# A gated linear attention with two expert stages on one core: VectorE's attention work of the first group behind the range reduction, and four smaller edits

## The chip, the core and the metric

The kernel runs on one core of a Trainium2 chip. The metric is the device time of one execution in microseconds (us). Five engines work side by side, each through its own queue in order: TensorE (PE in the profile, its weight loads as PEld), VectorE (DVE), ScalarE (ACT), GpSimd (POOL) and SyncE (SP, which issues most transfers). They meet through semaphores only.

## What is computed

Three stages follow each other: a linear attention with a decay for every key channel, an MLP with the gate h·cos(h), and a mixture of eight experts of which each token takes one. Queries, keys, values and decays are (4, 8, 768, 48); the MLP takes 3072 tokens of 384 channels to 2048 and back, an expert to 1024 and back.

```python
def _attn_ref(q, k, v, alpha):
    state = np.zeros((B, H, D, D))
    for t in range(S):
        state = alpha[:, :, t, :, None] * state + np.einsum('bhd,bhe->bhde', k[:, :, t], v[:, :, t])
        y[:, :, t] = np.einsum('bhd,bhde->bhe', q[:, :, t], state)

def _moe_ref(x, w_in, w_out):
    h = x @ w_in
    g = h * np.cos(h)
    return g @ w_out

def _moe2_ref(x, w_gate, w_output_gate, w1, w2):
    logits = x @ w_gate
    e_idx = np.argmax(logits, axis=1)
...
    for e in range(E):
        mask = e_idx == e
        h = np.maximum(x[mask] @ w1[e], 0.0)
        out[mask] = gate_w[mask, None] * eom[mask, e, None] * (h @ w2[e])
```

## The kernel before

**Units, groups and slots.** The sequence is cut into 6 chunks of 128 steps; with 4 batches this makes 24 units, u = 0 to 23, and four units with the same chunk form a group of 512 tokens. The MLP takes a group g in 16 slots, one for each block of 128 hidden channels, so there are 96 slots; J counts them from 0, and slot J belongs to group J // 16. While the MLP works on group g, the attention units of group g + 1 are computed between its steps. Units 0 to 4 are prepared by hand ahead of slot 0 (the head); "the first group" below is slots 0 to 15, in which units 5, 6 and 7 are prepared and in which VectorE also unpacks the 64-bit MLP weights.

**One slot.** The order is written out by hand. Slot J emits, in this order: the nine matmuls of `stage1` (L366, into `hp`, one of two PSUM buffers); place A; `nearest` (ScalarE, L373) and for the slot before `gated_halves` (ScalarE L391, GpSimd L392: `gh` and `gl`); place T; `turn` (VectorE L379, the range reduction, then ScalarE L380 and L381); place B; `gated` (VectorE L384, which frees `hp`); place P; the nine matmuls of `stage2` for slot J - 2 (L405, into `acc`); places C and D. The attention steps are put into these places by `at_slot(J, place, step, u)`; steps of one place run in the order of their registration, and each engine keeps the order in which its instructions were emitted.

**VectorE's attention steps of a unit.** `decay` (L142, L143: a scan of 128x520 that gives `w`), `recip` (L151, L152: a second scan), `k_left` and `k_right` (L169, L173), and `carry` (L184, which multiplies the stored total `wtot` into `dc`, and on ScalarE L186, which copies the new total over `wtot`). Unit 5 has its decay in slot 1 and its k steps and carry in slot 3, unit 6 in slots 4 and 6, unit 7 in slots 7 and 9. GpSimd multiplies the other halves of q (L160, L165) and scales the state (L193).

**Weight words.** In slots 0 to 13 `narrow` (place B, VectorE L334, L339, L343, each twice) makes fp32 words of two 128x384 blocks; in place A of the slot after, `halves` rounds each on ScalarE (L354) and subtracts on GpSimd (L355: `wil`, `wol`).

**The state update.** For units 0 to 19 `update` (L272) multiplies the transposed keys `ks` (128x112 weights) with four 128-column blocks of values; a block holds two heads of 48 columns, at columns 0 to 47 and 80 to 127, and 32 columns of zeros between them. Each of these fp32 matmuls stands twice in the trace.

**The experts.** An expert has 448 rows (the first: 256 early and then 192). `load_rows` loads them as tiles of 128 rows and a last one of 64, `rows_trans` (L629) transposes each tile in three column blocks, the last as 64x128 into 64 columns, and the products follow (L644, L658, L666). The next expert's `rows_trans` stands between the second products of the current one.

**Warming.** `warm(22)` issues 22 matmuls on zeros at the start, before the first unit's scores; `warm(9)` nine more between that unit's scores and its values.

Of the kernel before, what the change touches and what calls it, by code (L numbers as in the profile page):

```python
# [8 lines left out]
F32 = mybir.dt.float32  # L9
# [30 lines left out]
QO, KO, AO, VO = 0, 4 * C, 8 * C, 8 * C + 4 * 130 + 8  # L40
UCOL = VO + 4 * C
EARLY = 256
MAGIC = 1.5 * 2.0 ** 23
# [11 lines left out]
def kernel(  # L55
# [60 lines left out]

    def load_unit(u, parts=((0, UCOL),)):
        if u not in un:
            if u == B - 1:

                un[u] = tuple(x_p.tile([128, n], F32, tag=t, name="un") for n, t in ((AO, "xh"), (UCOL - AO, "xl")))
            else:
                t = u_p.tile([128, UCOL], F32, tag="un", name="un")
                un[u] = (t[:, 0:AO], t[:, AO:UCOL], t)
        for c0, c1 in parts:
            t, o = (un[u][2], 0) if len(un[u]) > 2 else (un[u][c0 // AO], c0 // AO * AO)
            nc.sync.dma_start(out=t[:, c0 - o:c1 - o], in_=units[u][:, c0:c1])

    def views(u):
# [4 lines left out]
            wt[u],  # L134
            av[:, VO - AO:].rearrange("p (a c) -> p a c", a=4),
        )
# [40 lines left out]
    def carry(u):  # L177
# [4 lines left out]
        if i > 0:  # L182
            dc_t[u] = d_p.tile([128, 4, 1], F32, tag="dc", name="dc")
            nc.vector.tensor_tensor(out=dc_t[u], in0=wb, in1=w[:, :, 64:65], op=ALU.mult)  # L184
        if i < NCH - 1:
            nc.scalar.copy(wb, w[:, :, 129:130])  # L186

# [78 lines left out]
    def update(u):  # L266
        if u // B == NCH - 1:
            return
        ks = sc_t[u][1]
        pp = (ps_a if u < B else ps_m).tile([128, 4, C], F32, tag="acc1" if u < B else "m", name="pp")  # L270
        for p in range(4):
            nc.tensor.matmul(  # L272
                out=pp[0:64 + D, p, :], lhsT=ks[:, p, :], rhs=views(u)[3][:, p, :],
                start=True, stop=True,
            )
        pp_t[u] = pp

    def update_out(u):
# [3 lines left out]
        pp = pp_t.pop(u)  # L282
        for p0, c0, v0 in ((0, 0, 0), (64, D, C - D)):
            m = state[b][p0:p0 + D, :, c0:c0 + D]
            pv = pp[p0:p0 + D, :, v0:v0 + D]
            if i == 0:
# [319 lines left out]
    def load_rows(e, r0, n, pool, tag):  # L606
# [9 lines left out]
        if rest:  # L616
            nc.vector.memset(xe[rest:128, full, DM:ROW], 0.0)
            after_sends(nc.sync.dma_start(out=xe[0:rest, full, :], in_=xs[r0 + full * 128:r0 + n, :]))
        return dict(e=e, n=n, tiles=tiles, xe=xe)

    def rows_trans(r, pool, th, tl):
# [3 lines left out]
        for k in range(KD):  # L625
            tp = ps_m.tile([128, 512], F32, tag="m", name="tp")[:, :n]
            for j, m in enumerate(r["tiles"]):
                o = j * 128
                nc.tensor.transpose(tp[:, o:o + m], r["xe"][0:m, j, k * 128:(k + 1) * 128], ident[0:m, 0:m])  # L629
            nc.scalar.copy(xh[:, k, :], tp)  # L630
# [100 lines left out]
    for u in range(GU, NU):  # L731
        J = NF * (u // GU - 1) + ((-2, 1, 4, 7) if u // GU == 1 else (-1, 2, 5, 7))[u % GU]
        at_unit[u] = J
        if u > GU:

            at_slot(max(J - 6, at_unit[u - 3] + 7 if u - 3 >= GU else 0), "A", load_unit, u)
            at_slot(J, "A", decay, u)
            at_slot(J, "D", q_right, u)
            at_slot(J, "B", recip, u)
            at_slot(J + 1, "D", q_left, u)  # L740
            at_slot(J + 2, "A", k_left, u, nc.vector)
            at_slot(J + 2, "A", k_right, u, nc.vector)
            at_slot(J + 2, "A", carry, u)
            at_slot(J + 2, "D", carry_state, u)
# [45 lines left out]
    with tc.manual_schedule():  # L790
        nc.scalar.activation(out=busy[:, 0:1], in_=halfpi, func=ACTF.Sin)
        warm(22)
        load_words(0, 0)
# [5 lines left out]
        def prepare(u):  # L799
# [6 lines left out]
            q_left(u, nc.vector)  # L806
            carry(u)

        prepare(0)
# [48 lines left out]
        k_right(4, nc.vector)  # L858
        carry(4)
        carry_state(4, nc.vector)  # L860
        nc.vector.tensor_copy(base, c_sb[:, CEB:CEB + E])
# [296 lines left out]
```

## Time and profile before

| | |
|---|---|
| median of 3 runs | 834.96 us (834.9 to 835.65) |
| the profiled execution | 836.24 us, of which the span from first to last instruction is 834.5 us |
| mean granted TensorE clock | 0.987 |
| busy share of the span: PE, PEld, DVE, ACT, POOL | 96%, 80%, 60%, 51%, 37% |

The profile shows one execution. Its own time is 1.28 us above the median, and 1.74 us of it lie outside of the span. A timeline row gives the start and the duration in us, the engine, the line, the operation, out<-in, the shape and the count of merged instructions, and in brackets the idle time ahead of it with what ended it. Matmul ends are modelled and overlap, so starts are what is compared there. The rows themselves stand below.

### The profile page before, as it was taken

The numbers are of one execution on the slowest core, as the hardware profiler recorded it, in microseconds if no ns is written. First come the engines' busy times: TensorE is split into PE (matmuls) and PEld (weight loads), VectorE is DVE, ScalarE is ACT, GpSimd is POOL, SyncE is SP. The second block draws the span as 40 slices with busy tenths as digits, with TensorE's granted clock in tenths as the row PEclk, the third lists the DMA queues.
The fourth block names the chain that finished last, engine by engine and source line by source line (L and its number), as shares of the span: only waits on it lengthen the run. The fifth ranks groups of instructions, "written<-read, shape, count | busy, mean of one in ns | idle before, by whom it ended". The sixth has DMA issues, their size and how long they took to land.

```text
span 834.5 us, 13942 instructions
## 1 busy us (share of the span) xinstructions
PE 797.1 (96%) x5415; PEld 671.7 (80%) x5415; DVE 500.4 (60%) x968; ACT 427.3 (51%) x782; POOL 311.4 (37%) x284
## 2 busy tenths in 40 slices
PE   8679799999999999999999999999999999999994
PEld 4457577788888888888878878889999999999994
DVE  7989998675467546763766335653764464454530
ACT  2355455754575457644665476564554453453420
POOL 3456557544355336443555333742000100101101
PEclk9998999999999999999999999999999999999998
DMA  9424443723201130123010002304753543533201
GB/s 336 162 98 165 165 165 105 256 59 113 73 2 52 71 122 0 52 70 123 1 52 30 30 1 77 115 1 146 232 160 104 166 140 110 167 123 117 78 11 36
DMA packets 46731, 85.22 MB, mean 102 GB/s; under 512 B 4136, under 2 KB 38216, under 8 KB 44096
## 3 DMA queue, kind: packets, MB, share of 16 engines
q1 hardware_dynamic: 43200, 74.67, 27.5%
q0 software_dynamic: 3456, 9.57, 3.1%
q8 instruction: 45, 0.74, 0.4%
q14 instruction: 30, 0.25, 0.1%
HBM read 69.01 MB, written 15.99 MB: 102 GB/s over the span
## 4 chain that ended last, share of the span: by engine, by line
PE 53%; issue 27%; DVE 10%; POOL 4%; ACT 2%; DMA 1%; POOLq 0%; SPq 0%; ACTq 0%; DVEq 0%
PE acc L405 21%; PE hp L366 21%; POOL out_dram L678 4%; DVE cv L334 2%; PE sc L200 2%; DVE cv L339 2%; PE yp L258 2%; PE yp L250 2%; PE pp L272 1%; DVE cv L343 1%; PE tp L429 1%; DVE t L384 1%; DVE w L143 1%; DVE t L379 1%; PE lp L461 1%
## 5 line engine op out<-in xcount | busy, mean ns | idle before, releaser
L392 POOL TENSOR_TENSOR gl<-t,gh 128x512 fp32r<-128x512 f32 x95 | 126.8, 1335 | 182.3 <-ACT gh L391 140.2
L373 ACT ACTIVATE t<-hp 128x512 f32<-128x512 f32 x96 | 57.3, 597 | 121.5 <-PE hp L366 110.6
L384 DVE TENSOR_TENSOR t<-hp,t 128x512 f32<-128x512 f32 x96 | 65.7, 684 | 88.1 <-ACT t L381 88.1
L379 DVE SCALAR_TENSOR_TENSOR t<-t,hp 128x512 f32<-128x512 f32 x96 | 65.7, 685 | 86.9 <-ACT t L373 86.6
L678 POOL DMA_INDIRECT out_dram<-ot,tk x32 | 30.9, 967 | 220.8 <-ACT ot L677 220.5
L658 PE MATMUL op<-h,hb 128*128 128x384 f32 x384 | 102.8, 340 | 0.0
L648 DVE SCALAR_TENSOR_TENSOR hb<-hp,hb 128x64 fp32r<-128x64 f32 (+3 forms) x136 | 45.3, 372 | 75.4 <-ACT hb L646 75.3
L405 PE MATMUL acc<-gh,woh 128*128 128x512 f32 x288 | 89.1, 416 | 0.0
L366 PE MATMUL hp<-xh,wih 128*128 128x512 f32 x288 | 84.3, 401 | 4.7 <-DVE t L384 2.9
L405 PE MATMUL acc<-gl,woh 128*128 128x512 f32 x288 | 84.4, 400 | 0.0
L405 PE MATMUL acc<-gh,wol 128*128 128x512 f32 x288 | 83.8, 399 | 0.0
L366 PE MATMUL hp<-xh,wil 128*128 128x512 f32 x288 | 83.5, 398 | 0.0
L366 PE MATMUL hp<-xl,wih 128*128 128x512 f32 x288 | 83.4, 398 | 0.0
L380 ACT ACTIVATE t<-t 128x512 f32<-128x512 f32 x96 | 60.7, 632 | 34.8 <-DVE t L379 34.8
L586 DVE TENSOR_TENSOR l<-raw,h 128x768 fp32r<-128x768 f32 x60 | 57.3, 957 | 32.5 <-ACT h L582 31.1
L646 ACT ACTIVATE hb<-hp 128x448 fp32r<-128x448 f32 (+2 forms) x72 | 36.3, 504 | 71.6 <-PE hp L644 71.5
L381 ACT ACTIVATE t<-t,halfpi 128x512 f32<-128x512 f32 x96 | 69.6, 725 | 3.1
L658 PEld LDWEIGHTS op<-h,hb 128*128 128x128 f32 x384 | 69.9, 188 | 0.5
L366 PEld LDWEIGHTS hp<-xh,wih 128*128 128x128 f32 x288 | 54.1, 190 | 19.6 <-DVE t L384 2.0
L366 PEld LDWEIGHTS hp<-xl,wih 128*128 128x128 f32 x288 | 54.7, 190 | 13.4
L405 PEld LDWEIGHTS acc<-gl,woh 128*128 128x128 f32 x288 | 54.7, 190 | 13.2
L366 PEld LDWEIGHTS hp<-xh,wil 128*128 128x128 f32 x288 | 54.5, 189 | 13.2
(139 smaller groups left out, 1501.6 us busy)
## 6 DMA issues: line engine op xcount, KB each, us to landing
raw<-in_w_dram SPq DMA_DIRECT2D x64, 384.0 KB, 3.2
un<-in_units_dram SPq DMA_DIRECT2D x20, 1032.0 KB, 5.1
raw<-in_w_in_dram SPq DMA_DIRECT2D x16, 384.0 KB, 3.6
raw<-in_w_out_dram SPq DMA_DIRECT2D x16, 384.0 KB, 4.0
xs<-zrow SPq DMA_DIRECT2D x8, 591.0 KB, 5.9
xe<-xs SPq DMA_DIRECT2D x7, 591.0 KB, 5.6
un<-in_units_dram SPq DMA_DIRECT2D x4, 512.0 KB, 6.0
un<-in_units_dram SPq DMA_DIRECT2D x4, 264.0 KB, 5.1
```

The costliest lines, as they stand in the source:

```text
L366: nc.tensor.matmul(out=hp, lhsT=w[:, k, fs], rhs=x[:, k, :], start=(n == 0), stop=(n == 3 * KD - 1))
L373: nc.scalar.activation(out=t, in_=hps[g, j], func=ACTF.Copy, bias=MAGIC)
L379: nc.vector.scalar_tensor_tensor(out=t, in0=t, scalar=MAGIC, in1=hp, op0=ALU.subtract, op1=ALU.subtract)
L380: nc.scalar.activation(out=t, in_=t, func=ACTF.Abs)
L381: nc.scalar.activation(out=t, in_=t, func=ACTF.Sin, scale=-TWO_PI, bias=halfpi)
L384: nc.vector.tensor_tensor(out=t, in0=hps.pop((g, j)), in1=t, op=ALU.mult)
L392: eng.tensor_tensor(out=gl, in0=gf, in1=gh.bitcast(F32), op=ALU.subtract)
L405: nc.tensor.matmul(out=acc[g][k], lhsT=w[:, j, ks], rhs=a, start=(j == 0 and n == 0), stop=(j == NF - 1 and n == 2),)
L586: (nc.vector.tensor_tensor if i < 4 else sub)(out=lo, in0=raws[i], in1=h.bitcast(F32), op=ALU.subtract)
L648: nc.vector.scalar_tensor_tensor(out=out_, in0=hp[:, c], scalar=0.0, in1=hh[:, c].bitcast(F32), op0=ALU.max, op1=ALU.subtract)
L658: nc.tensor.matmul(out=op, lhsT=a[:, sl], rhs=w[:, j, :], start=(j == 0 and i == 0), stop=(j == NEF - 1 and i == 2))
L678: sent = nc.gpsimd.indirect_dma_start(out=out, out_offset=bass.IndirectOffsetOnAxis(ap=tk[0:n, t, :], axis=0), in_=ot[0:n], in_offset=None ...
```

## The change

Five edits. **Place:** for units 5, 6 and 7 `decay`, `k_left`, `k_right` and `carry` move from place A to place B, that is from ahead of `turn` to right behind it; later groups keep place A. **Decay copy:** ScalarE's copy into `wtot` leaves `carry` and becomes `carry_keep`, for the planned units in place C of the same slot. **Warming:** `warm(22)` becomes `warm(17)`. **Update:** the value blocks are read as two pieces of 48 columns (a view of 160 columns in two strides of 80), so the matmul streams 96 columns for 128, and `pp` is 96 wide; the unit's tile grows by 32 unused columns, so that the last view fits. **Transposes:** the last tile of an expert is transposed as full 128x128 too; its rows 64 to 127 are set to zero over the full width of 394 columns, where before only 10 columns of them were.

```diff
--- before.py
+++ after.py
@@ -39,6 +39,8 @@
 
 QO, KO, AO, VO = 0, 4 * C, 8 * C, 8 * C + 4 * 130 + 8
 UCOL = VO + 4 * C
+
+UPAD = UCOL + C - 2 * D
 EARLY = 256
 MAGIC = 1.5 * 2.0 ** 23
 TWO_PI = 2.0 * math.pi
@@ -118,10 +120,10 @@
         if u not in un:
             if u == B - 1:
 
-                un[u] = tuple(x_p.tile([128, n], F32, tag=t, name="un") for n, t in ((AO, "xh"), (UCOL - AO, "xl")))
+                un[u] = tuple(x_p.tile([128, n], F32, tag=t, name="un") for n, t in ((AO, "xh"), (UPAD - AO, "xl")))
             else:
-                t = u_p.tile([128, UCOL], F32, tag="un", name="un")
-                un[u] = (t[:, 0:AO], t[:, AO:UCOL], t)
+                t = u_p.tile([128, UPAD], F32, tag="un", name="un")
+                un[u] = (t[:, 0:AO], t[:, AO:UPAD], t)
         for c0, c1 in parts:
             t, o = (un[u][2], 0) if len(un[u]) > 2 else (un[u][c0 // AO], c0 // AO * AO)
             nc.sync.dma_start(out=t[:, c0 - o:c1 - o], in_=units[u][:, c0:c1])
@@ -132,7 +134,7 @@
             qk[:, QO:QO + 4 * C].rearrange("p (a c) -> p a c", a=4),
             qk[:, KO:KO + 4 * C].rearrange("p (a c) -> p a c", a=4),
             wt[u],
-            av[:, VO - AO:].rearrange("p (a c) -> p a c", a=4),
+            av[:, VO - AO:UCOL - AO].rearrange("p (a c) -> p a c", a=4),
         )
 
     def decay(u):
@@ -182,8 +184,11 @@
         if i > 0:
             dc_t[u] = d_p.tile([128, 4, 1], F32, tag="dc", name="dc")
             nc.vector.tensor_tensor(out=dc_t[u], in0=wb, in1=w[:, :, 64:65], op=ALU.mult)
+
+    def carry_keep(u):
+        b, i = u % B, u // B
         if i < NCH - 1:
-            nc.scalar.copy(wb, w[:, :, 129:130])
+            nc.scalar.copy(wtot[b].rearrange("p (a c) -> p a c", c=1), views(u)[2][:, :, 129:130])
 
     def carry_state(u, eng=nc.gpsimd):
         b, i = u % B, u // B
@@ -267,10 +272,12 @@
         if u // B == NCH - 1:
             return
         ks = sc_t[u][1]
-        pp = (ps_a if u < B else ps_m).tile([128, 4, C], F32, tag="acc1" if u < B else "m", name="pp")
+        pp = (ps_a if u < B else ps_m).tile([128, 4, 2 * D], F32, tag="acc1" if u < B else "m", name="pp")
         for p in range(4):
+            o = VO - AO + p * C
+            v = un[u][1][:, o:o + 2 * (C - D)].rearrange("p (n c) -> p n c", n=2)[:, :, 0:D]
             nc.tensor.matmul(
-                out=pp[0:64 + D, p, :], lhsT=ks[:, p, :], rhs=views(u)[3][:, p, :],
+                out=pp[0:64 + D, p, :], lhsT=ks[:, p, :], rhs=v,
                 start=True, stop=True,
             )
         pp_t[u] = pp
@@ -280,9 +287,9 @@
         if i == NCH - 1:
             return
         pp = pp_t.pop(u)
-        for p0, c0, v0 in ((0, 0, 0), (64, D, C - D)):
+        for p0, c0 in ((0, 0), (64, D)):
             m = state[b][p0:p0 + D, :, c0:c0 + D]
-            pv = pp[p0:p0 + D, :, v0:v0 + D]
+            pv = pp[p0:p0 + D, :, c0:c0 + D]
             if i == 0:
                 nc.scalar.copy(m, pv)
             else:
@@ -614,7 +621,7 @@
             out=xe[:, 0:full, :], in_=xs[r0:r0 + full * 128, :].rearrange("(j p) c -> p j c", p=128)
         ))
         if rest:
-            nc.vector.memset(xe[rest:128, full, DM:ROW], 0.0)
+            nc.vector.memset(xe[rest:128, full, :], 0.0)
             after_sends(nc.sync.dma_start(out=xe[0:rest, full, :], in_=xs[r0 + full * 128:r0 + n, :]))
         return dict(e=e, n=n, tiles=tiles, xe=xe)
 
@@ -623,10 +630,11 @@
         xh = pool.tile([128, KD, n], F32R, tag=th, name="exh")
         xl = pool.tile([128, KD, n], F32R, tag=tl, name="exl")
         for k in range(KD):
-            tp = ps_m.tile([128, 512], F32, tag="m", name="tp")[:, :n]
-            for j, m in enumerate(r["tiles"]):
-                o = j * 128
-                nc.tensor.transpose(tp[:, o:o + m], r["xe"][0:m, j, k * 128:(k + 1) * 128], ident[0:m, 0:m])
+
+            tp = ps_m.tile([128, 512], F32, tag="m", name="tp")
+            for j in range(len(r["tiles"])):
+                nc.tensor.transpose(tp[:, j * 128:(j + 1) * 128], r["xe"][:, j, k * 128:(k + 1) * 128], ident)
+            tp = tp[:, :n]
             nc.scalar.copy(xh[:, k, :], tp)
             nc.vector.tensor_tensor(out=xl[:, k, :], in0=tp, in1=xh[:, k, :].bitcast(F32), op=ALU.subtract)
         r["x"] = (xh, xl)
@@ -734,13 +742,17 @@
         if u > GU:
 
             at_slot(max(J - 6, at_unit[u - 3] + 7 if u - 3 >= GU else 0), "A", load_unit, u)
-            at_slot(J, "A", decay, u)
+
+
+            pl = "B" if u // GU == 1 else "A"
+            at_slot(J, pl, decay, u)
             at_slot(J, "D", q_right, u)
             at_slot(J, "B", recip, u)
             at_slot(J + 1, "D", q_left, u)
-            at_slot(J + 2, "A", k_left, u, nc.vector)
-            at_slot(J + 2, "A", k_right, u, nc.vector)
-            at_slot(J + 2, "A", carry, u)
+            at_slot(J + 2, pl, k_left, u, nc.vector)
+            at_slot(J + 2, pl, k_right, u, nc.vector)
+            at_slot(J + 2, pl, carry, u)
+            at_slot(J + 2, "C", carry_keep, u)
             at_slot(J + 2, "D", carry_state, u)
         at_slot(J + 3, "P", scores, u)
         at_slot(J + 3, "C", masked, u, 0)
@@ -789,7 +801,7 @@
 
     with tc.manual_schedule():
         nc.scalar.activation(out=busy[:, 0:1], in_=halfpi, func=ACTF.Sin)
-        warm(22)
+        warm(17)
         load_words(0, 0)
         load_words(0, 1)
         load_words(0, 2)
@@ -805,6 +817,7 @@
             k_right(u, nc.vector)
             q_left(u, nc.vector)
             carry(u)
+            carry_keep(u)
 
         prepare(0)
         scores(0)
@@ -857,6 +870,7 @@
         k_left(4, nc.vector)
         k_right(4, nc.vector)
         carry(4)
+        carry_keep(4)
         carry_state(4, nc.vector)
         nc.vector.tensor_copy(base, c_sb[:, CEB:CEB + E])
         nc.vector.tensor_copy(tri16, c_sb[:, CT:CT + 128])
```

**VectorE, slots 3 and 4** (`t<-t,hp` is `turn`, `t<-hp,t` is `gated`, `cv` are the words of `narrow`). Before, from behind slot 2's `gated` on:

```order
L169 TENSOR_TENSOR un<-un,w 128x4x64
L173 TENSOR_TENSOR un<-un 128x4x64
L184 TENSOR_TENSOR dc<-wtot_126,w 128x4
L379 SCALAR_TENSOR_TENSOR t<-t,hp 128x512
L334 TENSOR_SCALAR cv<-raw 128x384 x2
L339 SCALAR_TENSOR_TENSOR cv<-raw,cv 128x384 x2
L343 SCALAR_TENSOR_TENSOR cv<-raw,cv 128x384 x2
L384 TENSOR_TENSOR t<-hp,t 128x512
L304 SCALAR_TENSOR_TENSOR xl<-yp,xh 128x3x128
L142 MEMSET scan_120 128x8
L143 SCALAR_TENSOR_TENSOR w<-un,scan_120 128x520
```

Of the changed kernel, from the same place:

```order
L386 SCALAR_TENSOR_TENSOR t<-t,hp 128x512
L171 TENSOR_TENSOR un<-un,w 128x4x64
L175 TENSOR_TENSOR un<-un 128x4x64
L186 TENSOR_TENSOR dc<-wtot_126,w 128x4
L341 TENSOR_SCALAR cv<-raw 128x384 x2
L346 SCALAR_TENSOR_TENSOR cv<-raw,cv 128x384 x2
L350 SCALAR_TENSOR_TENSOR cv<-raw,cv 128x384 x2
L391 TENSOR_TENSOR t<-hp,t 128x512
L311 SCALAR_TENSOR_TENSOR xl<-yp,xh 128x3x128
L386 SCALAR_TENSOR_TENSOR t<-t,hp 128x512
L144 MEMSET scan_120 128x8
L145 SCALAR_TENSOR_TENSOR w<-un,scan_120 128x520
```

The k steps and `dc` of unit 5 now stand behind `turn` of slot 3, and the memset and scan of unit 6 behind `turn` of slot 4.

**ScalarE, from slot 3 to the start of slot 4** (`wih`, `woh` are the rounded weights, `t<-hp` is `nearest`). Before:

```order
L186 COPY wtot_126<-w 128x4
L354 CAST wih<-cv 128x3x128
L354 CAST woh<-cv 128x384
L373 ACTIVATE t<-hp 128x512
L391 CAST gh<-t 128x512
L380 ACTIVATE t<-t 128x512
L381 ACTIVATE t<-t,halfpi 128x512
L303 ACTIVATE xh<-yp 128x3x128
L354 CAST wih<-cv 128x3x128
L354 CAST woh<-cv 128x384
```

Of the changed kernel:

```order
L361 CAST wih<-cv 128x3x128
L361 CAST woh<-cv 128x384
L380 ACTIVATE t<-hp 128x512
L398 CAST gh<-t 128x512
L387 ACTIVATE t<-t 128x512
L388 ACTIVATE t<-t,halfpi 128x512
L310 ACTIVATE xh<-yp 128x3x128
L191 COPY wtot_126<-w 128x4
L361 CAST wih<-cv 128x3x128
L361 CAST woh<-cv 128x384
```

The copy into `wtot` went from ahead of slot 3's weight casts and `nearest` to the slot's end.

**TensorE, an expert's transposes** between its second products. Before:

```order
L629 MATMUL tp<-c_sb,xe 128x128 x3
L629 MATMUL tp<-c_sb,xe 128x64
L629 MATMUL tp<-c_sb,xe 128x128 x3
L629 MATMUL tp<-c_sb,xe 128x64
L629 MATMUL tp<-c_sb,xe 128x128 x3
L629 MATMUL tp<-c_sb,xe 128x64
L658 MATMUL op<-h_5169,hb 128x384
```

Of the changed kernel:

```order
L674 MATMUL op<-l_5165,hb 128x384
L636 MATMUL tp<-c_sb,xe 128x128 x12
L666 MATMUL op<-h_5164,hb 128x384
L666 MATMUL op<-l_5165,hb 128x384
L666 MATMUL op<-h_5164,hb 128x384 x2
```

Twelve transposes of one shape stand where three runs of three were each followed by a smaller one.

## Rows read from the trace of the kernel before

**Rows 1.** The page: the span.

```profile
span 834.5 us, 13942 instructions
```

**Rows 2.** Stretches: busy of PE, PEld, DVE, ACT, POOL (instructions); granted clock, DMA share, GB/s.

```profile
54.30:108.30 54.00, 43.65 (x299) 34.33 (x297) 49.01 (x86) 26.56 (x53) 32.59 (x29) 0.91 0.41 142
...
108.30:135.00 26.70, 26.03 (x176) 20.79 (x176) 25.84 (x45) 16.75 (x31) 16.31 (x15) 1.00 0.57 199
...
152.00:480.00 328.00, 328.00 (x2595) 265.82 (x2595) 194.51 (x365) 184.84 (x331) 153.57 (x134) 1.00 0.19 65
585.00:815.00 230.00, 229.45 (x1236) 215.06 (x1236) 116.09 (x255) 104.27 (x189) 26.00 (x27) 1.00 0.41 126
```

**Rows 3.** The same view: two stretches with a lower granted clock.

```profile
38.13:41.54 3.41, 3.41 (x9) 2.22 (x7) 3.37 (x7) 1.95 (x5) 1.80 (x2) 0.50 0.31 83
...
96.16:99.57 3.41, 3.41 (x10) 2.67 (x9) 3.41 (x8) 1.77 (x3) 1.37 (x2) 0.50 0.91 372
```

**Rows 4.** Timeline of the head.

```profile
7.08 0.89 DVE L165 TENSOR_TENSOR un<-un 128x252 f32<-128x252 f32 x1
...
7.40 1.84 PEld L717 LDWEIGHTS <-busy 128*128 128x128 bf16 x9 [0.27 <-issue]
...
10.86 1.29 DVE L219 TENSOR_TENSOR at<-sc,mask 128x512 f32<-128x512 f32 x2 [1.58 <-PE sc L200]
```

**Rows 5.** Timeline from the end of slot 5 into slot 6.

```profile
76.93 0.68 DVE L384 TENSOR_TENSOR t<-hp,t 128x512 f32<-128x512 f32 x1
...
78.38 0.20 ACT L186 COPY wtot<-w 128x4 f32<-128x4 f32 x1 [2.67 <-DVE dc L184]
...
79.94 0.69 DVE L379 SCALAR_TENSOR_TENSOR t<-t,hp 128x512 f32<-128x512 f32 x1 [1.59 <-ACT t L373]
```

**Rows 6.** Timeline of slot 12, a slot with no step in place A.

```profile
120.52 0.69 DVE L379 SCALAR_TENSOR_TENSOR t<-t,hp 128x512 f32<-128x512 f32 x1 [0.47 <-ACT t L373]
```

**Rows 7.** Timeline of slot 4.

```profile
63.60 1.00 POOL L355 TENSOR_TENSOR wol<-cv,woh 128x384 fp32r<-128x384 f32 x1
...
63.61 2.08 DVE L143 TENSOR_TENSOR_SCAN w<-un,scan 128x520 f32<-128x520 f32 x1
64.56 2.21 POOL L392 TENSOR_TENSOR gl<-t,gh 128x512 fp32r<-128x512 f32 x1
...
66.43 1.44 DVE L152 TENSOR_TENSOR_SCAN un<-un,scan 128x520 f32<-128x520 f32 x1
```

**Rows 8.** Timeline of slot 1.

```profile
41.69 0.60 ACT L373 ACTIVATE t<-hp 128x512 f32<-128x512 f32 x1 [1.56 <-PE hp L366]
```

**Rows 9.** Timeline of slot 17.

```profile
150.69 0.14 PEld L429 LDWEIGHTS tp<-c_sb,xh 128*128 128x128 f32 x1 [0.32 <-ACT xh L418]
```

**Rows 10.** Timeline: an update and what follows; then weight loads by form: busy, mean ns, idle before.

```profile
215.05 1.04 PE L272 MATMUL pp<-un,ks 128*112 128x128 f32 x8
215.85 0.71 PE L405 MATMUL acc<-gh,woh 128*128 128x512 f32 x2
...
L366 PEld LDWEIGHTS hp<-xh,wil 128*128 128x128 f32 x288 | 54.5, 189 | 13.2
...
L258 PEld LDWEIGHTS yp<-at,un 128*32 128x32 f32 x768 | 21.5, 110 | 4.5 <-DVE at L219 4.1 <-issue 0.4
L272 PEld LDWEIGHTS pp<-un,ks 128*112 128x112 f32 x160 | 19.9, 176 | 6.5 <-ACT ks L224 4.2 <-issue 0.6
```

**Rows 11.** Timeline of an expert's transposes, and of twelve full-size ones.

```profile
620.83 2.05 PE L629 MATMUL tp<-c_sb,xe 128*128 128x128 f32 x12
622.81 0.45 PE L658 MATMUL op<-h,hb 128*128 128x384 f32 x1
...
565.02 1.61 PE L429 MATMUL tp<-c_sb,xh 128*128 128x128 f32 x12
566.47 0.18 PE L504 MATMUL rp<-oh,tri 128*128 128x32 bf16 x1
```

**Rows 12.** Timeline of the start: a memset of 128x520.

```profile
0.93 0.49 DVE L704 MEMSET scan<- 128x520 f32 x1 [0.93 <-PEq L1147]
```

## The prediction

> **What bounds the kernel now.** I read the span [rows 1] and then the table by stretches [rows 2]. From 152 us on TensorE never stands: 328.00 us busy of 328.00, and 229.45 of 230.00 in the experts. There every column or idle gap taken from TensorE shortens the span, and what VectorE does is covered (194.51 of 328.00, 116.09 of 230.00). From 54.3 to 108.3 us it is the other way round: VectorE is busy 49.01 of 54.00 us and TensorE 43.65, so a slot lasts as long as VectorE's row with its waits. From 108.3 to 135 us both are full (25.84 and 26.03 of 26.70). So there are three accounts: the head, the first group by VectorE, and the rest by TensorE.
>
> **Warming, five matmuls fewer.** The last nine warming loads start within 7.40 to 9.24 us, 0.20 us each [rows 4], and five of them are 1.0 us. The last operand of the first scores that VectorE makes is ready at 7.08 + 0.89 = 7.97 us, and VectorE then idles 1.58 us until those scores are there [rows 4]. The gap is longer than the piece cut out, so all of 1.0 us should move on through the head, in which VectorE goes from one unit to the next; **-1.0 us**, with 0 and -1.1 as ends. The five are those at the faster pace, behind the point at which the clock is up, so no slower matmul is added.
>
> **The decay copy and the k steps, slots 3, 6 and 9.** In slot 6 `gated` starts at 76.93 and `turn` at 79.94 us, 3.01 us later, and VectorE idles 1.59 us of that for ScalarE's `nearest` [rows 5]. ScalarE is late because its copy into `wtot` waits 2.67 us for `dc`, that is for VectorE's k steps, and the weight casts and `nearest` are queued behind the copy. In slot 12, with nothing in place A, the same wait is 0.47 us [rows 6]. With the copy at the slot's end and the k steps behind `turn`, slots 3, 6 and 9 should wait as slot 12 does: 1.59 - 0.47 = 1.1 us less each. The k steps themselves (some 0.8 us) are moved, not removed. They now stand where GpSimd runs `wil`, `wol` and `gl`, and rows of slot 4 show what that means [rows 7]: the scan that is issued at 63.61, just behind `wol` at 63.60, takes 2.08 us and ends 1.1 us behind `wol`, and `gl` then takes 2.21 us. One waits for the other, instruction by instruction. But the unpacking that followed `turn` before already waited for the same GpSimd work; the k steps take its place in that wait. I price the contention as unchanged; if it is all new, it eats the 1.1 us, which is the other end. In slot 9 TensorE may be late too: the clock was at 0.50 from 96.16 to 99.57 us [rows 3], which is where `hp` of slot 9 is made, so I take 0.7 there. Sum: **-2.9 us**, from 0 to -3.3.
>
> **The decays, slots 1, 4 and 7.** In slot 4 the scan stood ahead of `turn` and spent its first 0.9 us waiting for `wol` [rows 7]. Behind `turn` it is issued about 0.7 us later and still finds `wol` only just done, so it ends where it did; the second scan (66.43, 1.44 us) then waits for `gl`, which ends at 64.56 + 2.21 = 66.77 us, as before. Slots 4 and 7: 0. Slot 1 is different. There ScalarE's `nearest` waits 1.56 us for TensorE's `hp` [rows 8], because TensorE runs at half clock from 38.13 us [rows 3]; the scan fills that wait now, and behind `turn` it will not. That costs up to 1.4 us, and nothing if the clock comes back in time; **+0.7 us**.
>
> **Slot 17.** The same copy stands ahead of `nearest` there, and two transposes wait for ScalarE's copies out of `acc`, one of them 0.32 us in the weight load [rows 9], the other about as much. With `nearest` some 0.7 us earlier and the copy's own 0.2 us behind, about 0.5 us of both goes: **-0.5 us**. In the later groups the copy blocks ScalarE too, but TensorE does not stand, so it is worth 0.
>
> **The update.** Eight fp32 matmuls (four, each twice) take 215.85 - 215.05 = 0.80 us, 0.10 each [rows 10]. If the moving columns set this, 96 for 128 saves a quarter, 0.2 us. If the weight loads do, it saves less: a load lasts 110 ns for 32 columns, 176 for 112 and 189 for 128, so 0.8 ns per column, and the 112 columns are 0.09 us of streaming, nearly the whole 0.10. I lean to the loads, since their slope is the nearest row, and take 0.06 us. Units 8 to 19 do it in the TensorE-bound part, 12 times: **-0.7 us**, from 0 to -2.4; units 0 to 7 lie under VectorE. The Trainium skill, page "TensorE: Matmul & The Clock Gate", section "LDWEIGHTS (loading the stationary operand)", puts a load at its columns divided by 1.2 ns, whatever its rows; 112 columns are 93 ns by that, and it speaks against a full quarter here. The slope of the three rows agrees with it; taken as the floor of a matmul's spacing, it would leave an estimate of 12 x 8 x 7 ns = 0.7 us.
>
> **The transposes.** Twelve, of which three are 64-row tiles, take 622.81 - 620.83 = 1.98 us; twelve full ones elsewhere take 566.47 - 565.02 = 1.45 us [rows 11]. So the small tiles cost more than full ones, 0.53 us in an expert. Seven experts give 3.7 us, and the first one's later rows, with three small tiles among six, about the same 0.5: **-4.2 us**. The ends are -5.2 (the spacing within a run of full tiles is a little lower) and 0 (if the step to the next PSUM tile, not the tile's height, is what costs). They stand on TensorE between second products, with TensorE full [rows 2]. The wider memset replaces a small one; one of 128x520 took 0.49 us [rows 12], it is issued an expert ahead, and VectorE is half idle there: 0. Without that cover it would cost 8 x 0.4 us.
>
> **Sum.** -1.0 - 2.9 + 0.7 - 0.5 - 0.7 - 4.2 = -8.6 us, so the profiled span of 834.5 would be 825.9 and its 836.24 us would be 827.6. The median, 834.96, lies 1.28 us under the profiled execution; from it, **826.4 us**. Differences below 0.2% (1.7 us) can hardly be told from no change here.
>
> **The rivals.**
> (a) The first group gives nothing. For it: the k steps meet GpSimd's row, TensorE is full from 108 us on and may hold the slots where VectorE no longer does, and slot 1 loses its cover. Against it: the idle 1.59 us has one clear cause. Then -1.0 - 0.7 - 4.2 = -5.9: 829.1 us.
> (b) Everything at its good end: moving columns set the update (-2.4), the clock is back in slots 1 and 9 (-3.3, 0), transposes -5.2. With the head and slot 17, -12.4: 822.6 us. For it: the spacing within a run of transposes; against: the slope of the loads.
> (c) The transposes gain nothing. For it: the three groups of an expert also change PSUM tile. Against it: the twelve full ones change it too and are faster. Then -4.4: 830.6 us.
> (d) Slower: the clock. It fell to 0.50 in the first 100 us [rows 3], and these stretches lay in the part that VectorE paces. If the new order shifts TensorE's idle gaps so that the clock falls in the stretch where TensorE is full, each us at 0.50 there costs half a us. It decides from 2 x 8.6 = 17 us at the lower level; 21 us give 836.9. In the three stretches from 108 us on the clock is 1.00 [rows 2], so this is unlikely.
> (e) The change does not do what it says, because VectorE's waits for GpSimd and not ScalarE's copy set the slots: that is (a) in its price.
>
> **How the numbers follow.** Forecast (group gains between half and full) 0.55; (a) with (e) 0.20; (b) 0.12; (c) 0.08; (d) 0.03; no visible change from a mix of losses 0.02. The range takes in (a) and the near side of (b): 822.8 to 829.6 us. Faster by over 0.2% is the forecast, (a), (b) and (c), 0.95; I give 0.94 to that, 0.03 to within 0.2% and 0.03 to slower.
>
> **What would show it.** Per step: the first scores 1.0 us earlier; in slots 3, 6 and 9 about 1.9 us from `gated` to `turn` less, with VectorE's idle before `turn` near 0.5 us, and the copy into `wtot` without its wait; in slots 4 and 7 the same length as before; in slot 1 an idle VectorE ahead of `turn`; eight update matmuls in 0.6 to 0.75 us; twelve transposes in 1.3 to 1.5 us. Wrong would be slots 3, 6 and 9 as long as before, longer waits in the unpacking, or transposes of 1.9 us.

## The result, and the profile after

The changed kernel takes 824.31 us (median of 4 runs, 824.0 to 827.59) where the kernel before takes 835.26 us beside it; the ratio is 0.988, 95% interval 0.985 to 0.990. In a second set of runs the same kernel measured 827.14 us (5 runs, 823.52 to 827.71) against 835.5: 0.989, 0.987 to 0.991. The nine runs lie on two levels, four at 823.5 to 824.5 with a mean granted clock of 0.987 to 0.989, and five at 827.1 to 827.7 with 0.982 to 0.985; a section below shows, for one execution of each level, which slots make the 3 us. The forecast was 826.4 us, 822.8 to 829.6.

The profiled execution took 824.48 us; its page's span answers [rows 1]:

```profile
span 822.6 us, 13914 instructions
```

The stretches that answer [rows 2], moved to the same work (busy time of PE, PEld, DVE, ACT and POOL with their instructions, then granted clock, DMA share and GB/s):

```profile
54.00:104.00 50.00, 42.33 (x331) 33.48 (x324) 48.25 (x84) 25.98 (x50) 32.30 (x28) 0.96 0.44 154
104.00:131.00 27.00, 25.85 (x180) 20.73 (x179) 26.16 (x47) 17.40 (x32) 16.24 (x15) 1.00 0.56 196
148.00:476.00 328.00, 328.00 (x2601) 265.81 (x2601) 195.79 (x366) 184.81 (x332) 153.56 (x134) 1.00 0.19 66
580.00:803.00 223.00, 222.70 (x1233) 214.18 (x1234) 116.02 (x254) 102.44 (x188) 26.38 (x27) 1.00 0.43 131
```

The three accounts still hold: VectorE paces the first stretch (48.25 of 50.00 us), TensorE the last two. Set against each other work by work, the two traces give the ledger of the profiled pair:

| place | shift of the changed kernel, us | its own part |
|---|---|---|
| `gated` of slot 0 | -0.46 | head -0.5 |
| `gated` of slot 10 | -2.70 | first group -2.2 |
| `turn` of slot 19 | -3.44 | slot 17 -0.9, then +0.1 |
| `turn` of slot 95 | -4.61 | updates -1.2 |
| last matmul | -11.62 | experts -7.0 |
| last instruction | -11.85 | end -0.2 |

**Slot 6**, `gated` of slot 5 to the copy, answers [rows 5]:

```profile
76.58 0.68 DVE L391 TENSOR_TENSOR t<-hp,t 128x512 f32<-128x512 f32 x1
...
77.73 0.69 DVE L386 SCALAR_TENSOR_TENSOR t<-t,hp 128x512 f32<-128x512 f32 x1 [0.48 <-ACT t L380]
...
80.62 0.20 ACT L191 COPY wtot<-w 128x4 f32<-128x4 f32 x1 [0.40 <-DVE dc L186]
```

VectorE waits 0.48 us for `nearest` where it waited 1.59, the value of slot 12 in [rows 6], and the copy waits 0.40 us at the slot's end, with nothing urgent queued behind it. From one `gated` to the next, slots 3, 6 and 9 fall from 8.13, 8.16 and 8.15 us to 7.00, 6.97 and 6.98. Slots 4 and 7 stay at 8.23 and 8.25.

**Slot 1** answers [rows 8]:

```profile
41.17 0.60 ACT L380 ACTIVATE t<-hp 128x512 f32<-128x512 f32 x1 [1.50 <-PE hp L373]
...
41.80 0.69 DVE L386 SCALAR_TENSOR_TENSOR t<-t,hp 128x512 f32<-128x512 f32 x1 [2.07 <-ACT t L380]
...
42.54 2.20 DVE L145 TENSOR_TENSOR_SCAN w<-un,scan 128x520 f32<-128x520 f32 x1
```

`hp` comes as late as before (1.50 us of waiting on ScalarE, 1.56 before), but the scan now stands behind `turn`, and VectorE idles 2.07 us. The slot takes 9.88 us for 8.52.

**Slot 17** answers [rows 9]: the three weight loads of the transposes are one row without idle time, and the slot takes 3.63 us for 4.49.

```profile
146.13 1.56 ACT L425 ACTIVATE xh<-acc 128x512 f32<-128x512 f32 x3
...
147.55 0.34 PEld L436 LDWEIGHTS tp<-c_sb,xh 128*128 128x128 f32 x3
```

**An update and an expert's transposes** answer [rows 10, 11], each with the product that follows: 0.71 us for 0.80, and 1.23 us for 1.98.

```profile
211.34 0.93 PE L279 MATMUL pp<-un,ks 128*112 128x96 f32 x8
212.05 0.72 PE L412 MATMUL acc<-gh,woh 128*128 128x512 f32 x2
```

```profile
614.76 1.47 PE L636 MATMUL tp<-c_sb,xe 128*128 128x128 f32 x12
...
615.99 0.42 PE L666 MATMUL op<-h,hb 128*128 128x384 f32 x1
```

### The profile page after: what moved, and what is told of

Same layout as the page of the kernel before. It is cut to its first block, busy times and chain, and to the rows that moved or that the text cites. A ratio compares the mean times of both kernels' runs of the same rounds, so it can differ in the third digit from the quotient of the medians.

```text
span 822.6 us, 13914 instructions
## 1 busy us (share of the span) xinstructions
PE 786.5 (96%) x5410; PEld 669.1 (81%) x5410; DVE 501.6 (61%) x968; ACT 425.4 (52%) x782; POOL 308.4 (37%) x284
## 4 chain that ended last, share of the span: by engine, by line
PE 54%; issue 27%; DVE 9%; POOL 4%; ACT 1%; DMA 1%; POOLq 0%; SPq 0%; ACTq 0%; DVEq 0%
PE acc L412 22%; PE hp L373 21%; POOL out_dram L686 4%; PE sc L205 2%; DVE cv L341 2%; PE yp L263 2%; PE yp L255 2%; DVE cv L346 2%; PE pp L279 1%; DVE cv L350 1%; PE tp L436 1%; DVE w L145 1%; DVE t L391 1%; PE lp L468 1%; PE kp L216 1%
```

## The experiments

All times, and the length of five slots in the profiled execution of each (from `gated` of the slot before to `gated` of the slot, us). A ratio is to the kernel before in the same set.

| kernel | median, us (runs) | ratio, 95% | slot 1 | 3 | 6 | 9 | 17 |
|---|---|---|---|---|---|---|---|
| before | 835.3 to 835.9 | | 8.52 | 8.13 | 8.16 | 8.15 | 4.49 |
| changed | 824.31 (4) | 0.9878, 0.9852 to 0.9903 | 9.88 | 7.00 | 6.97 | 6.98 | 3.63 |
| changed, second set | 827.14 (5) | 0.9889, 0.9870 to 0.9909 | 10.88 | 6.98 | 6.98 | 9.07 | 3.64 |
| e1 transposes | 829.09 (6) | 0.9926, 0.9909 to 0.9942 | 8.57 | 8.14 | 8.17 | 8.14 | 4.48 |
| e2 copy and place | 833.86 (7) | 0.9969, 0.9957 to 0.9980 | 9.99 | 7.00 | 6.98 | 7.81 | 3.63 |
| e3 copy alone | 832.88 (6) | 0.9959, 0.9945 to 0.9974 | 8.56 | 7.04 | 7.05 | 8.34 | 3.64 |
| e4 warming alone | 837.34 (12) | 1.0011, 0.9996 to 1.0026 | 9.21 | 8.14 | 8.15 | 8.14 | 4.47 |
| e5 place alone | 834.46 (10) | 0.9981, 0.9969 to 0.9992 | 9.98 | 6.98 | 6.97 | 6.98 | 4.48 |
| e6 update alone | 835.37 (12) | 0.9988, 0.9977 to 1.0000 | 8.55 | 8.12 | 8.16 | 8.15 | 4.47 |
| e7 changed, decay of unit 5 back | 824.09 (5) | 0.9855, 0.9841 to 0.9870 | 8.47 | 6.98 | 6.99 | 6.99 | 3.62 |
| e8 changed, update of 48 columns | 825.46 (4) | 0.9869, 0.9850 to 0.9888 | 10.78 | 6.98 | 6.98 | 6.97 | 3.63 |
| e9 changed, short tiles last | 826.60 (4) | 0.9901, 0.9883 to 0.9920 | 10.62 | 7.00 | 6.98 | 6.98 | 3.63 |
| e10 as e7, warming of 22 | 824.39 (4) | 0.9872, 0.9857 to 0.9888 | 8.33 | 6.98 | 6.99 | 6.97 | 3.64 |
| e11 changed, all ahead of `turn` | 824.61 (4) | 0.9863, 0.9846 to 0.9881 | 8.47 | 7.05 | 7.03 | 7.04 | 3.63 |

### e1, the transposes alone

```diff
-            tp = ps_m.tile([128, 512], F32, tag="m", name="tp")[:, :n]
-            for j, m in enumerate(r["tiles"]):
-                o = j * 128
-                nc.tensor.transpose(tp[:, o:o + m], r["xe"][0:m, j, k * 128:(k + 1) * 128], ident[0:m, 0:m])
+            tp = ps_m.tile([128, 512], F32, tag="m", name="tp")
+            for j in range(len(r["tiles"])):
+                nc.tensor.transpose(tp[:, j * 128:(j + 1) * 128], r["xe"][:, j, k * 128:(k + 1) * 128], ident)
+            tp = tp[:, :n]
...
```

> The kernel before with the change of the transposes alone (full 128-row tiles, the wider memset). Theory one, the tile's height: every step between a 128-row and a 64-row tile holds TensorE, so twelve full transposes take about 1.2 us for 2.0 in each of seven experts, the first expert's six lose about 0.75 us too, and the whole is 6.0 us shorter (829.3 where the kernel before is at 835.3). Theory two, the step to the next PSUM tile costs and not the height: 1.98 us as before and no change of the time. Theory three, part of the gain is only free because the first group moved the rest too: 3 to 4 us.

6.2 us less by the ratio (4.8 to 7.6). In its profile the last matmul is 7.36 us earlier than in that of before and `turn` of slot 95 0.48 us, so 6.9 us lie in the experts, as in the changed kernel (7.0). Theory one holds; the gain needs nothing from the first group.

### e2, e3 and e5: the copy and the place, together and apart

```diff
 # e3: the copy alone
-            nc.scalar.copy(wb, w[:, :, 129:130])
...
+            at_slot(J + 2, "C", carry_keep, u)
...
 # e5: the place alone, the copy right behind carry
-            at_slot(J, "A", decay, u)
...
+            pl = "B" if u // GU == 1 else "A"
+            at_slot(J, pl, decay, u)
...
-            at_slot(J + 2, "A", carry, u)
...
+            at_slot(J + 2, pl, carry, u)
+            at_slot(J + 2, pl, carry_keep, u)
...
```

e2 has the place of e5 and the copy of e3.

> The kernel before with the decay copy at its new place and the SBUF work of the first group behind turn, nothing else. Theory: slots 3, 6 and 9 1.1 us shorter each, slot 17 0.9 us shorter, slot 1 1.4 us longer: 2.9 us less, 832.4 where before is at 835.3. Rival, the loss in slot 1 belongs to the head's new timing (warming) and not to the decay's place: slot 1 as long as before, 4.2 us less.

> The kernel before with the decay copy alone at its new place (the slot's end); decays and k steps of the first group stay ahead of turn. Theory one, what held the slots was ScalarE's queue behind the copy: slots 3, 6 and 9 1.1 us shorter each, slot 17 0.9 us, and slot 1 keeps its length because its decay stays: 4.2 us less, 831.1 where before is at 835.3, better than copy and place together. Theory two, with the k steps ahead of turn VectorE reaches turn 0.8 us later whatever ScalarE does: slots 3, 6 and 9 lose only 0.3 us each, slot 17 still 0.9, 1.8 us less in all.

> The kernel before with the first group's decays and k steps behind turn; the decay copy is issued right behind them, as before, in every group. Theory one, what counts is only that ScalarE's copy no longer stands ahead of nearest, and in the first group the place does that as well as the copy's own move: the intervals from gated to gated 2 to 3, 5 to 6 and (if the clock is up) 8 to 9 fall from 8.13 to 7.0 us, 0 to 1 grows by 1.4, and 16 to 17 stays at 4.49 because the later groups are untouched; about 2 us less in all at best, 833.5 where before is at 835.5. Theory two, the copy behind the k steps holds ScalarE at its new place too: 2 to 3 at 8.1 and no gain, 836.9 with the loss of slot 1.

The table settles three points. Slots 3 and 6 fall to 7.0 us with the copy alone, with the place alone and with both, so it is one gain that either edit takes: the copy no longer stands ahead of `nearest` on ScalarE. Slot 17 falls only where the copy is moved (e2, e3), not in e5, whose weight loads still wait as in [rows 9]:

```profile
148.06 0.14 PEld L433 LDWEIGHTS tp<-c_sb,xh 128*128 128x128 f32 x1 [0.32 <-ACT xh L422]
...
148.55 0.14 PEld L433 LDWEIGHTS tp<-c_sb,xh 128*128 128x128 f32 x1 [0.35 <-ACT xh L422]
```

And slot 1 is 1.4 us longer only where the decay is moved (e2, e5). The rival of e2 falls with that, and so do the second theories of e3 and e5. In e3 the k steps do stand ahead of `turn`, which starts 3.78 us behind `gated`, with no idle time of VectorE between (of its rows in between, only `dc` is shown):

```profile
75.64 0.68 DVE L388 TENSOR_TENSOR t<-hp,t 128x512 f32<-128x512 f32 x1
...
78.01 1.47 POOL L396 TENSOR_TENSOR gl<-t,gh 128x512 fp32r<-128x512 f32 x1
...
78.25 1.25 DVE L185 TENSOR_TENSOR dc<-wtot,w 128x4 f32<-128x4 f32 x1
...
79.42 0.67 DVE L383 SCALAR_TENSOR_TENSOR t<-t,hp 128x512 f32<-128x512 f32 x1
```

The slot is still 7.05 us: what counts is that VectorE does not idle, not where in its row `turn` stands. The `dc` row is a product of four columns that lasts 1.25 us and ends, at 79.50, with GpSimd's `gl` (79.48); in the changed kernel the same instruction takes 0.15 us, and `k_right` ahead of it 1.52 for 1.23. What went wrong in my expectation of e3 is slot 9, 8.34 us: TensorE's clock was at 0.50 from 91.72 to 98.54 us there, as from 94.43 to 97.84 in e2 (7.81), and in both the slot waits for TensorE (`nearest` waits 2.33 us for `hp` in e3 and 1.04 in e2). So e3 is not shown to be better than e2; the two intervals overlap.

### e4, the warming alone

```diff
-        warm(22)
+        warm(17)
```

> The kernel before with 17 warming matmuls for 22, nothing else. Theory one, the head is a chain: the first scores 1.0 to 1.4 us earlier and the whole as much. Theory two, TensorE's clock falls to 0.50 again in the head as in the changed kernel and takes back about half: the first scores 1.4 us earlier, the first turn and the whole 0.5 us. Theory three, nothing is left of it behind the first group: 0.

No gain: 1.0011 (0.9996 to 1.0026). Its profile:

```profile
5.70 1.67 PEld L721 LDWEIGHTS <-busy 128*128 128x128 bf16 x8 [0.28 <-issue]
...
7.90 1.00 PEld L204 LDWEIGHTS sc<-un 64*128 64x128 f32 x16 [0.53 <-POOL un L170]
```

The warming is over before the operands are there, and the first scores wait 0.53 us for GpSimd's product: in this execution the clock came up at about 5.8 us, and the warming no longer reaches to where the operands are ready. Over all profiles, seven with 17 and seven with 22, the first scores come at 8.30 us in the mean against 9.15. From there to `gated` of slot 0 eleven of the fourteen take 29.84 to 29.86 us, so the head hands a lead on whole. The other three, the changed kernel, e8 and e11, all with 17, take 30.74 to 30.86; they are the ones in which a stretch at 0.50 begins at 26.3 to 27.3 us. In the mean, 0.43 us of lead are left at slot 0 (38.56 against 38.99). In e4's own profile the lead is still whole there (37.78 us for 39.50), and slot 1, with the clock at 0.50 from 33.12 to 39.95 us, gives 0.7 us of it back (9.21 for 8.52).

The runs show the rest. Five of e4's twelve took 834.7 to 835.3 us with a mean granted clock of 0.987 to 0.989; the fastest of the nineteen runs of the kernel before in this set took 835.2. The other seven took 837.1 to 839.9 us with 0.981 to 0.984, a clock that one of the nineteen shows. So with 17 the kernel is slightly faster where the clock holds, and in this set the clock fell more often; why it did is not shown. Theory three is nearest for the whole time, and theory two names what takes the lead back.

### e6 and e8: the update

```diff
 # e6: of the kernel before
...
-                out=pp[0:64 + D, p, :], lhsT=ks[:, p, :], rhs=views(u)[3][:, p, :],
+                out=pp[0:64 + D, p, :], lhsT=ks[:, p, :], rhs=v,
...
 # e8: of the changed kernel
-            v = un[u][1][:, o:o + 2 * (C - D)].rearrange("p (n c) -> p n c", n=2)[:, :, 0:D]
+            v = un[u][1][:, o:o + D]
...
```

> The kernel before with 96 moving columns for 128 in the update alone. Theory one, the weight load of 112 columns sets the spacing: eight matmuls from 0.80 to 0.72 us, twelve units in the part that TensorE sets, 1.0 us less, 834.6 where before is at 835.6. Theory two, the moving columns set it: 0.60 us and 2.4 us less. Theory three, 0.

> The changed kernel with 48 moving columns in the update for 96: it leaves out the product of each pair's second head, and gives that head the first one's. Theory one, the weight load of 112 columns is the floor: the eight matmuls stay 0.098 us apart (0.72 us to the next product), and the time stays at 824.3. Theory two, the columns still count: 0.05 us apart and 12 x 8 x 0.049 = 4.7 us less, 819.6.

e6 gains 1.0 us by the ratio (0 to 1.9); between slots 19 and 70 its profile moves 1.2 us ahead. e8 halves the columns once more, its time agrees with the changed kernel's within the intervals, and its timeline reads the same, 0.71 us to the next product:

```profile
212.66 0.89 PE L279 MATMUL pp<-un,ks 128*112 128x48 f32 x8
213.37 0.94 PE L412 MATMUL acc<-gh,woh 128*128 128x512 f32 x3
```

The starts of its single matmuls stand 0.098 us apart, as with 96 columns; only the first of the eight follows its columns (0.042 us with 48, 0.082 with 96). With 128 the spacing was 0.109. So the moving columns are not the floor, and theory one holds. That the floor is the weight load is argued from its 112 columns, since no run changed them; other rows agree with it: with weights of 128 columns the first expert's products start 0.111 us apart at 192 moving columns and 0.119 at 256, later ones 0.203 at 448. The slope from 256 to 448 would put 192 at 0.09 us (an estimate), so there too a floor shows, and a higher one. By the spacings of the update its floor is met at about 115 columns (0.098 / 0.109 of 128, an estimate): of the 32 columns cut some 13 paid.

### e9, the short tiles last

```diff
+        for small in (False, True):
+            for k in range(KD):
+                for j, m in enumerate(r["tiles"]):
+                    if (m < 128) == small:
+                        o = j * 128
+                        nc.tensor.transpose(tps[k][:, o:o + m], r["xe"][0:m, j, k * 128:(k + 1) * 128], ident[0:m, 0:m])
...
```

> The changed kernel with the short tiles back as 64-row transposes, but each expert's three short ones issued together behind its nine full ones. Theory one, the step between the two heights holds TensorE, about 0.095 us into the short tile, as much out of it and 0.05 to 0.11 on the next: one visit for an expert in place of three leaves a third of the 0.75 us, 1.48 us for the twelve against 1.23, 8 x 0.25 = 2.0 us more than the changed kernel (826.2). Theory two, each short transpose costs that by itself: 1.98 us again and 6 us more (830).

```profile
615.05 1.47 PE L638 MATMUL tp<-c_sb,xe 128*128 128x128 f32 x12
...
616.45 0.44 PE L669 MATMUL op<-h,hb 128*128 128x384 f32 x1
```

1.40 us for twelve, against 1.23 with full tiles and 1.98 with three separate short ones. The single starts show where it goes. Before, each short tile started 0.204 us behind the full one ahead of it (full to full: 0.109), the full one behind it again 0.204 us later, and the next 0.165. In e9 the step in costs the same 0.204, and the short ones then follow each other at 0.112 and 0.064 us, together less than two full ones (0.218). The change of height costs, not the short tile, and theory one holds. The same step stands elsewhere in the kernel before: behind an update, whose weights have 128 rows, the first scores matmul (64 rows) starts 0.203 us after the last one, and a transpose of 112 rows 0.109. By its ratio e9 lies 0.1% above the changed kernel of its set, inside the interval; the verdict rests on the rows.

### e7, e10, e11 and the changed kernel again: slot 1, and the level of the time

```diff
 # e7
-            at_slot(J, pl, decay, u)
+            at_slot(J, "A" if u == GU + 1 else pl, decay, u)
 # e10: that, and
-        warm(17)
+        warm(22)
 # e11
-            pl = "B" if u // GU == 1 else "A"
+            pl = "A"
```

> The changed kernel with one piece taken back: the decay of unit 5 (slot 1) stands ahead of turn again; its k steps and everything else as changed. Theory one, that scan had filled VectorE's wait for ScalarE's nearest, which waits for a TensorE at half clock, and behind turn it costs its whole length: the interval from gated 0 to gated 1 goes back from 9.88 to 8.5 us and the kernel is 1.4 us shorter, 822.9. Theory two, slot 1 is long because the head's clock changed: it stays at 9.9, and 824.3. Theory three, the slot is shorter but the next ones give it back, since TensorE is full from slot 10 on: less than 0.5 us.

> The changed kernel itself once more, beside the three others of this set, so that they can be compared with it on one chip. Both theories of the other runs expect 824.0 to 824.5, with some runs 1 to 3 us above where the clock falls to 0.50 at another place in the first 100 us.

> The changed kernel with unit 5's decay ahead of turn and with 22 warming matmuls. Theory one, five warming matmuls fewer bring nothing in the whole time, since the clock that falls in the head takes it back: the same as with 17 (824.09 measured before, 822.85 in its profiled execution), 1.2 us less than the changed kernel where the clock falls alike. Theory two, the warming is worth its 1.0 us: 1.0 us slower than with 17, 824 to 825.

> The changed kernel with all of the first group's VectorE work ahead of turn again, decays and k steps; the decay copy at its new place, the transposes, the update and the warming as changed. Theory one, the copy alone gives the gain of slots 3, 6 and 9, and the place only costs slot 1: 0 to 1 at 8.5 us, 2 to 3, 5 to 6 and 8 to 9 at 7.0 to 7.1, and 1.2 us less than the changed kernel, 823.0. Theory two, the k steps ahead of turn hold VectorE where TensorE comes late, as 8 to 9 at 8.34 with the copy alone: about the changed kernel's time, 824.2.

(The changed kernel again is e12.) In e7 the scan fills the wait again, and slot 1 takes 8.47 us:

```profile
38.69 1.60 DVE L145 TENSOR_TENSOR_SCAN w<-un,scan 128x520 f32<-128x520 f32 x1
...
40.08 0.60 ACT L380 ACTIVATE t<-hp 128x512 f32<-128x512 f32 x1 [1.50 <-PE hp L373]
...
40.70 0.69 DVE L386 SCALAR_TENSOR_TENSOR t<-t,hp 128x512 f32<-128x512 f32 x1 [0.41 <-ACT t L380]
```

Over all profiles slot 1 takes 9.9 to 10.9 us with the decay behind `turn` and 8.3 to 8.6 ahead of it (9.2 in e4): 1.4 to 2.4 us, the price of one piece of the change in that slot. Not all of it reaches the end of the group: in e7, e10 and e11 slot 5 takes 6.77, 6.95 and 6.66 us for the changed kernel's 6.21, with the clock at 0.50 and `nearest` waiting 0.7 to 1.0 us for TensorE. In e7:

```profile
60.31:67.14 6.83, 6.29 (x24) 5.20 (x25) 6.71 (x12) 2.32 (x4) 5.28 (x4) 0.50 0.72 271
```

From `gated` of slot 0 to that of slot 15 the three take 99.34 to 99.41 us for 100.19, some 0.8 us less. e10 and e11 agree with e7 in the slots of the table and, within their intervals, in the time; neither the five warming matmuls nor the place of the k steps shows, but an effect of 1 us (0.12%) would lie inside these intervals. e7 has the lowest ratio of all, 0.9855; it beats the kernel before clearly, and the changed kernel by 0.2 to 0.3% in its middle, with intervals that overlap or touch. That it is better is shown for slot 1, and not quite for the whole time.

e12 fell on the upper level of the times (its profiled execution took 827.71 us, 3.2 above the first), and its profile shows why:

```profile
35.53:42.36 6.83, 6.13 (x21) 4.80 (x23) 3.99 (x11) 3.94 (x9) 2.70 (x5) 0.50 0.35 112
62.84:69.67 6.83, 5.53 (x22) 4.59 (x23) 6.72 (x11) 3.08 (x6) 5.70 (x4) 0.50 0.71 271
93.56:100.39 6.83, 6.12 (x17) 5.00 (x18) 6.09 (x12) 3.64 (x7) 4.58 (x6) 0.50 0.79 284
```

The first execution had these instead, and 1.00 at that place in slot 9:

```profile
27.32:30.73 3.41, 2.83 (x31) 2.16 (x24) 2.65 (x6) 0.89 (x2) 0.97 (x2) 0.50 0.72 242
37.56:40.97 3.41, 3.41 (x9) 2.28 (x7) 2.17 (x5) 2.07 (x5) 1.69 (x2) 0.50 0.29 61
51.21:54.63 3.42, 3.42 (x44) 2.53 (x46) 3.42 (x6) 1.77 (x3) 1.92 (x2) 0.50 0.32 124
64.87:68.28 3.41, 3.41 (x10) 2.63 (x9) 3.34 (x5) 0.52 (x1) 3.21 (x2) 0.50 0.93 377
...
93.80:100.80 7.00, 7.00 (x80) 5.51 (x79) 6.53 (x13) 4.65 (x9) 4.75 (x6) 1.00 0.86 316
```

What follows in e12's slot 9:

```profile
101.94 0.60 ACT L380 ACTIVATE t<-hp 128x512 f32<-128x512 f32 x1 [2.30 <-PE hp L373]
...
102.57 0.69 DVE L386 SCALAR_TENSOR_TENSOR t<-t,hp 128x512 f32<-128x512 f32 x1 [2.88 <-ACT t L380]
```

VectorE idles 2.88 us behind a TensorE at 0.50, and the slot takes 9.07 us for 6.98; slot 1 adds 1.0 us. These two are 3.1 of the 3.3 us between the spans. Code and data are the same; where the clock falls in the first 100 us differs between these two executions, and it costs where TensorE is what a slot waits for. Whether the shorter warming puts five of the nine runs on the upper level is not shown: e7, with 17, has none of five at or below 0.984, and e10, with 22, one of four.

## Why the prediction was right, and where it was not

- **Warming, -1.0: wrong.** The step that failed is "The gap is longer than the piece cut out, so all of 1.0 us should move on through the head". The gap was read in one execution, in which the clock came up late (the slow pace of [rows 4] ends at 7.40 us; in the other profiles at 5.1 to 8.2); over all profiles the first scores come 0.85 us earlier. The head does hand a lead on, but the sum had no term for the clock: a stretch at 0.50 took 0.9 us back in the profiled execution and left -0.46, and seven of e4's twelve runs, with a lower mean clock, took 837.1 us and more. Alone the edit is worth nothing that can be measured (e4). Five loads are 1.08 us rather than 1.0, since their starts stand 0.216 us apart; that changes little.
- **Copy and k steps, -2.9: right in mechanism, nearly so in size.** The waits fell to what slot 12 shows, 1.13 to 1.19 us for each slot, 3.5 in all. The doubt about slot 9 was justified: it gives all in seven of the ten profiles that have one of the two edits, and 0.3, -0.2 and -0.9 us in the others, with the clock at 0.50 at about the place that I had named. That both edits were needed was my silent assumption; either does it. The k steps did meet GpSimd's row (2.4 us in slot 6 for 0.97), and the first pair of the unpacking behind them was shorter (1.25 us for 2.12); from `turn` on the slot grew by 0.67 us, so contention as unchanged was a fair price.
- **The decays: 0 in slots 4 and 7 was right, +0.7 in slot 1 too small.** It measured +1.4, and +2.4 in the execution with the longer stretch at 0.50. The bound of 1.4 was the right number for the slot; halving it for a clock that might be back in time was hope. In the three executions with that decay back ahead of `turn`, some 0.8 us of it is left by slot 15, so the whole time sees less.
- **Slot 17, -0.5: -0.86 measured.** Both waits of the transposes went, as said; they are 0.67 us (0.32 and 0.35 in e5), where I had taken off the copy's own 0.2. The last 0.2 us I did not trace.
- **Update, -0.7: -1.2 measured, the mechanism right.** A floor of 0.098 us, most likely the load, took over from the columns. I subtracted 7 ns from a spacing that I had rounded to 0.10; it was 0.109, and the first of the eight gains 0.028 besides. The Trainium skill, page "TensorE: Matmul & The Clock Gate", section "LDWEIGHTS (loading the stationary operand)", puts a load at its columns divided by 1.2 ns, an estimate of 93 ns for 112 columns. The 0.098 us that stay from 96 to 48 moving columns are near it.
- **Transposes, -4.2: -7.0 measured, outside of its own ends (-5.2 and 0).** The mechanism was right, the price low. The comparison row, twelve full transposes in 1.45 us [rows 11], holds pauses of 0.08 and 0.06 us in front of its tenth and its eleventh; and I compared starts up to the product without seeing that the short last tile delays that product by 0.17 us too. Twelve in a row take 1.23: 0.75 us for an expert, 6.1 us with the first expert's six. The other 0.9 us is the second point of the last section, which no row of before showed. The Trainium skill, page "TensorEngine Tiling (Array Packing)", section "Key Properties", says that a change of the tiling mode drains TensorE. That a 64-row transpose is such a change is my reading; the trace agrees so far that a start behind a change of height comes 0.095 us later, in and out.
- **The sum**, -8.6 us, fell 3.2 us short of the profiled pair's -11.8. Errors of opposite sign cancel in part: the head 0.5 and slot 1 0.7 us too good, and 4.3 us too little for the transposes (2.8), slots 3, 6 and 9 (0.6), the update (0.5) and slot 17 (0.4). The median of the first set lies 2.1 us under the forecast, that of the second 0.7 above; the second is nearer by luck, because most of its runs fell on the upper level, for which the sum had no term.
- **Rivals.** (c) falls by e1 and e9, (e) by e3 and e5. (a) was half right in its parts, slot 1 and the late TensorE, and wrong in that they eat everything. (b)'s end for the transposes was passed. (d) named the clock, but the place where it acted is the head and the part that VectorE paces. Once, in e6, a stretch of 3.41 us at 0.50 did fall where TensorE is full:

```profile
585.37:588.78 3.41, 3.41 (x19) 3.41 (x18) 1.30 (x5) 1.38 (x3) 0.00 (x0) 0.50 0.64 204
```

That execution took 836.34 us, 1 us above its kernel's median.

## What to carry to other kernels

Look at what is queued behind a small instruction that waits: a copy of four columns cost 1.1 us in each of three slots and 0.9 us in slot 17, and in the three slots moving it in its own queue was as good as moving the work that it waits for. Keep work that fills a wait where it is; in the slot itself its removal costs up to the whole wait. Where a kernel's clock falls at varying places, read a gap in several executions before counting on it, and price a row by the spacing of its instructions, not by the length of a block with a pause in it.

## What the runs showed of the hardware

- A step between 128-row and 64-row tiles holds TensorE 0.095 us each way, and 0.05 us more on the second transpose behind the way out; a product that follows a short tile directly starts 0.15 to 0.20 us behind it, where one that follows a full tile starts after 0.03.
- In three of the experts 0.28 us more went outside of the transposes. The 72 matmuls of `e_stage1` (448 columns) run 0.2044 us apart in three experts of every profile, and in the other four 0.2066 or 0.2027, each pace over a whole expert. In the kernel before and e2 to e6, with separate short tiles, all of these four are at the slower pace; in the seven profiles with full tiles one of 28 is (in the changed kernel); in e9, with the short tiles last, three of four. So the pace goes with the short tiles; how they set it was not tried and stays open.
- The granted clock falls to 0.50 at other places in the two profiled executions of the changed kernel, in the first 100 us (once, in e6, later; behind the last matmul it falls in every profile). TensorE is busy 42.33 of 50.00 us from 54 to 104 us. It moves the whole time by some 3 us here, about what the copy alone is worth (3.4 us by e3's ratio).
- While GpSimd's subtraction `gl` ran, a VectorE product of four columns took 1.25 us instead of 0.15 and ended with it (e3).
